# Column sums of w_mod from its natural 112-row chunks, a new order of work up to the first sums over tokens, and small VectorE operations set apart

## The chip, the cores and the metric

The kernel runs on one core of a Trainium2 chip. The metric is the device time of one execution in microseconds (us); lower is better. The engines are TensorE (PE in the profile; PEld is its weight load), VectorE (DVE), ScalarE (ACT), GpSimd (POOL) and SyncE (SP), which issues most of the loads. Each engine has its own list of instructions and works through it in order; semaphores make one engine wait for another.

## The reference

An adaLN-conditioned block: linear attention, then an MLP that mixes tokens. S = 2048 tokens, D = 448 channels, 16 heads of 28, F = 1792.

```
mod = silu(c) @ w_mod                     # w_mod: 448 x 2688, six vectors of 448
sa, ca, ga, sb, cb, gb = mod in six parts
h = layernorm(x) * (1 + ca) + sa
q, k, v = h @ wqkv                        # 448 x 1344
phi(t) = where(t > 0, t + 1, exp(t)) + 1e-6
kv = sum over tokens of phi(k) v;  z = sum over tokens of phi(k)
x = x + ga * ((phi(q) kv) / (phi(q) z + 1e-6)) @ wo
h = layernorm(x) * (1 + cb) + sb
x = x + gb * (gelu(h^T @ w1 + b1) @ w2 + b2)^T
```

## The kernel before

All is float32. TensorE's fast format, fp32r, keeps fewer bits, so most operands are cut into a high and a low half (ScalarE makes the high half by a copy, VectorE the low half by a subtraction) and a product is three matmuls: high by high, high by low, low by high. The order of each engine's instructions is the order in which the program writes them; it was laid out by hand, and nothing reorders it.

**Tiles.** The tokens are 16 tiles t of 128. `XT[t]` is a tile transposed (channels on the partitions, `load_xt`), `X[t]` the tile as it is (`load_x`). Channels come in chunks of 128, 128, 128 and 64. All big tiles come from one pool of 74 slots ("slots").

**The start.** Layernorm is folded into the weights: for the projections the raw x is multiplied by the weight rows scaled with 1 + ca, and the mean is taken off by an additional row. So the first thing that is needed is column j = 1 of `mod`, channels on the partitions: `col[1]`. The program loads c, then `w_mod`'s part for j = 1 in four blocks of rows (`load_first`, L148 to 152: 128, 128, 128 rows, and the last 64 rows folded in two halves, 128 x 256, laid out by the host in an input of its own). While the loads are under way TensorE runs nine matmuls on ones (`keep_warm(WARM)`, L181). `silu(c)` is made by ScalarE and VectorE (L187 to 191). `col_mm` (L218, L220) multiplies a block by silu(c), repeated, and so sums over its rows: five instructions for a set of 448 columns. For j = 1 it runs on block 0 and block 1, and then on the sum `acc` of blocks 2 and 3, which VectorE has made (`col_acc`, L204 and L211). Five more matmuls on ones follow (`keep_warm(5)`). `col_out` (L226) takes the result out of the PSUM bank. For j = 0, later, VectorE folds all four blocks (L206, L208, L211) and `col_mm` runs once.

**Weights.** `w_high` (L256, `wh`) scales a chunk of the k weights with `col[1]` and rounds it; `w_low` (L268, `wl`) makes the low half. `w_row`, `row_part` (L274, L276), `row_sum` (L283), `row_bias` (L286) and `row_out` (L290, L291) make the rows that stand for the mean and for sa.

**Projections.** `a_split(t)` cuts `XT[t]` into `hh` (L400) and `hl` (L403). `project(t, 1)` is ten matmuls (L420, `kp`): three each for chunks 0 to 2, one for chunk 3, whose low parts lie in the free half of the partitions. For tiles 0 and 1 the twenty matmuls are in an order of their own (`projects`). `close(t)` (L427) adds the rows of mean and rest, for which the tile's statistics must have been transposed (`a_rows` L383 and L385, `a_transpose` L393, `a_copy` L396).

**Statistics.** Mean and variance of a tile come either from ScalarE in two passes (`a_stats_act`, L351 and L330) or from VectorE (`a_stats_dve`, L367 and L368); GpSimd makes the powers (`a_pow`, L342). Before the change tiles 0 to 3 are ScalarE's.

**Sums over tokens.** `a_exp` (L434, L435) and `a_pk` (L440) make phi(k); `a_pk_parts` cuts it into `pkh` (L488) and `pkl` (L490, or for most tiles L492 with an adding DMA from GpSimd, L493). `a_norm`, `a_high`, `a_low` make the normalized tile in two halves `xh`, `xl`. `a_outer(t)` (L514, `cacc`) adds a tile's products to four PSUM banks: eleven matmuls, of which seven use `pkh` and four `pkl`.

**Order around the change.** After the start the program is a straight list by hand down to a loop over t = 4 to 15, in which each step projects tile t + 1, closes tile t, adds tile t - 4 to the sums, makes statistics three tiles ahead, cuts `XT[t + 3]`, and does a piece of the q weights and of `mod`. SyncE's loads are in one list too: c, w_mod for j = 1, xt0, the k weights, xt1, xt2, w_mod for j = 0, then x and xt in turns with the q weights between tile 5 and tile 6.

Of the kernel before, what the change touches and what calls it, by code (L numbers as in the profile page):

```python
# [8 lines left out]
F32 = mybir.dt.float32  # L9
# [41 lines left out]
def block_kernel(ctx: ExitStack, tc: tile.TileContext, x, xt, wqkv, wo, w1, b1, w2, b2, c, wmod, wfirst, out):  # L51
# [67 lines left out]
    c_sb = cst.tile([P, 8], F32, name="c_sb")  # L119
    nc.sync.dma_start(c_sb, c)  # L120
    X = [None] * NT
# [11 lines left out]
    wm = {}  # L133

    def load_mod(j):
        for k in range(4):
            wm[j, k] = (tslot if j == 5 else slot)(f"wm{j}_{k}", parts=G)
            nc.sync.dma_start(wm[j, k], wmod[k * G:(k + 1) * G, j * D:(j + 1) * D])

# [8 lines left out]
    def load_first(j):  # L148
        for k in range(4):
            w = D if k < 3 else 256  # L150
            wm[j, k] = slot(f"wm{j}_{k}", w)
            nc.sync.dma_start(wm[j, k], wfirst[j, :, k * D:k * D + w])
# [9 lines left out]
    load_x(1)  # L162
# [6 lines left out]
    load_qkv(0)  # L169
    load_xt(6)  # L170
    load_x(6)
    for t in (7, 8):
        load_xt(t)
        load_x(t)
# [11 lines left out]
    ec = cst.tile([P, 8], F32, name="ec")  # L186
    nc.scalar.activation(ec, c_sb, AF.Exp, scale=-1.0)  # L187
    sc = cst.tile([P, 8], F32, name="sc")
    nc.vector.tensor_scalar_add(ec, ec, 1.0)
    nc.vector.reciprocal(ec, ec)  # L190
    nc.vector.tensor_mul(sc, c_sb, ec)
    mods, macc = {}, {}
# [6 lines left out]
    one = ones[:, 0:1]  # L199

    def col_acc(j):
        acc = macc[j] = slot(f"acc{j}")
        if j:
            nc.vector.tensor_scalar_mul(acc, wm[j, 2], sc[:, 2:3])  # L204
        else:
            nc.vector.tensor_scalar_mul(acc, wm[j, 0], sc[:, 0:1])  # L206
            for k in (1, 2):
                nc.vector.scalar_tensor_tensor(acc, wm[j, k], sc[:, k:k + 1], acc, op0=ALU.mult, op1=ALU.add)  # L208
        for r, (c0, c1) in enumerate(((0, 256), (256, D))):
            p = slice(r * 64, (r + 1) * 64)  # L210
            nc.vector.scalar_tensor_tensor(acc[p, c0:c1], wm[j, 3][p, :c1 - c0], sc[p, 3:4], acc[p, c0:c1],  # L211
                                           op0=ALU.mult, op1=ALU.add)

    def col_mm(ps, a, b, first, last):
        b = b.to_broadcast([P, P])
        for ch in range(4):
            n = P if ch < 3 else 64
            nc.tensor.matmul(ps[:n, ch * P:(ch + 1) * P], a[:, ch * P:ch * P + n], b, start=first and ch == 0,  # L218
                             stop=last, skip_group_check=True)
        nc.tensor.matmul(ps[64:, 384:512], a[:, 384:D], b, start=False, stop=last, skip_group_check=True)  # L220

    def col_out(j, ps):
        col[j] = cst.tile([P, 4], F32, name=f"col{j}")
        ps = ps.rearrange("p (c n) -> p c n", n=P)[:, :, 0]
        if j == 1:
            nc.vector.tensor_scalar_add(col[j], ps, 1.0)  # L226
        else:
            nc.vector.memset(col[j], 0.0)
            nc.vector.tensor_copy(col[j][:, :3], ps[:, :3])
            nc.vector.tensor_copy(col[j][:64, 3:4], ps[:64, 3:4])  # L230

    def mod_part(j, k):
        if k == 0:
            macc[j] = (tslot if j == 5 else slot)(f"acc{j}", parts=G)
            nc.vector.tensor_scalar_mul(macc[j], wm[j, 0], sc[:G, 4:5])
        else:
            nc.vector.scalar_tensor_tensor(macc[j], wm[j, k], sc[:G, 4 + k:5 + k], macc[j], op0=ALU.mult, op1=ALU.add)
# [88 lines left out]
    junk = slot("junk")  # L326
# [35 lines left out]
    def a_stats_dve(ts):  # L362
        g, ve = a_group(ts)

        def one(i):
            b6 = small.tile([P, 6], F32, name=f"st{ts[i]}", tag="st")
            nc.vector.bn_stats(b6, X[ts[i]])  # L367
            nc.vector.bn_aggr(mv[ts[i]][:, 0:2], b6)  # L368
# [4 lines left out]
        return one, end  # L373

    def a_stats(t):
        one, end = a_stats_dve((t,))
        one(0)
        end()

    def a_rows(t):  # L380
        r = rowst[t % RING]
        pair = mv[t][:, 0:2]
        nc.vector.tensor_copy(r[:, 64:].rearrange("p (b c) -> p b c", b=2)[:, :, 0:2],  # L383
                              pair.unsqueeze(1).to_broadcast([P, 2, 2]))
        nc.vector.tensor_sub(r[:, 66:68], pair, r[:, 64:66].bitcast(F32))  # L385
# [46 lines left out]
    def a_exp(t, ps):  # L432
        eks[t] = (slot(f"ek{t}"), slot(f"rk{t}"))
        nc.scalar.activation(eks[t][0], ps, AF.Exp, scale=mv[t][:, 2:3])  # L434
        nc.scalar.activation(eks[t][1], ps, AF.Relu, scale=mv[t][:, 2:3])  # L435
# [69 lines left out]
    def a_outer(t):  # L505
        if not cacc:
            cacc.extend(bank(f"cacc{ch}") for ch in range(4))
        xh, xl = xss.pop(t)
        kh, kl = pks.pop(t)
        for ch in range(4):  # L510
            s = slice(ch * P, (ch + 1) * P)
            todo = [(xh, kh), (xh, kl)] + ([(xl, kh)] if ch < 3 else [])
            for i, (a, b) in enumerate(todo):
                nc.tensor.matmul(cacc[ch][:, :D], a[:, s], b, start=(t == 0 and i == 0),  # L514
                                 stop=(t == NT - 1 and i == len(todo) - 1))

    pc = bank("col1")
    for k in range(2):
        col_mm(pc, wm[1, k], sc[:, k:k + 1], k == 0, False)
    nc.scalar.activation(sel_s, sel_f, AF.Copy)  # L520
    col_acc(1)
    a_split(0)
    col_mm(pc, macc.pop(1), one, False, True)
    keep_warm(5)
    col_out(1, pc)
    for ch in (3, 0, 1, 2):
        w_high(1, ch)
        w_low(1, ch)
    a_split(1)
    a_split(2)  # L530
    projects([(0, "hh", 0), (0, "hl", 0), (0, "hh", 3), (0, "hh", 1), (0, "hl", 1), (0, "wl", 0), (0, "hh", 2),
              (0, "hl", 2), (0, "wl", 1), (1, "hh", 0), (1, "hh", 1), (1, "hh", 2), (1, "hh", 3), (0, "wl", 2),
              (1, "wl", 0), (1, "wl", 1), (1, "wl", 2), (1, "hl", 0), (1, "hl", 1), (1, "hl", 2)], 1, "kp")
    project(2, 1, "kp")
    w_row(1)
    act01, end01 = a_stats_act((0, 1))
    act01(0)
    col_acc(0)
    pc = bank("col0")
    col_mm(pc, macc.pop(0), one, True, True)  # L540
    row_sum(1)
    a_split(3)
    act01(1)
    end01()
    col_out(0, pc)
    for ch in range(4):
        row_part(1, ch)
    a_rows(0)
    a_rows(1)
    project(3, 1, "kp")  # L550
    a_transpose(0, 2)
    row_bias(1)
    a_split(4)
    a_norm(0)
    dve45, end45 = a_stats_dve((4, 5))
    dve45(0)
    act23, end23 = a_stats_act((2, 3))
    act23(0)
    act23(1)
    end23()  # L560
    a_copy(0)
    a_copy(1)
    row_out(1)
    a_rows(2)
    a_rows(3)
    a_high(0)
# [5 lines left out]
    project(4, 1, "kp")  # L572
    a_split(5)
    a_low(0)
    kps = [close(t, 1) for t in (0, 1)]
    a_transpose(2, 2)
    project(5, 1, "kp")
    a_exp(0, kps[0])
    a_pk(0, kps[0])
    dve45(1)  # L580
    end45()
    a_copy(2)
    a_copy(3)
    kps += [close(t, 1) for t in (2, 3)]
    a_exp(1, kps[1])
    a_norm(1)
    a_pk_parts(0)
    a_outer(0)
    a_pk(1, kps[1])
    a_rows(4)  # L590
    a_rows(5)
    a_transpose(4, 2)
    a_exp(2, kps[2])
    a_split_high(6)
    a_pk(2, kps[2])
    a_split_low(6)
    a_exp(3, kps[3])
    a_high(1)
    a_copy(4)
    a_copy(5)  # L600
    project(6, 1, "kp")
    kps.append(close(4, 1))
    a_stats(6)
    a_pk_parts(1)
    a_low(1)
    a_rows(6)
    a_pk(3, kps[3])
    a_pk_parts(2)
    a_stats(7)
    wo_sb = []  # L610
    late = [t for t in range(NT) if t not in Q_EARLY.values()]
    for t in range(4, NT):
# [12 lines left out]
        if t == 12:  # L625
            mp = mod_sum2(2)
        if 4 < t < NT - 2:
            a_rows(t + 2)
        if 5 <= t < 9:
            w_low(0, t - 5)  # L630
            row_part(0, t - 5)
        if 7 < t + 3 < NT:
            a_stats(t + 3)
# [4 lines left out]
        if t + 3 < NT:  # L638
            a_split_high(t + 3)
# [6 lines left out]
        if t + 3 < NT:  # L646
# [524 lines left out]
_INS = ['A_x', 'xt', 'qkv', 'A_wo', 'B_w1', 'b1', 'B_w2', 'b2', 'c', 'B_wmod', 'first']  # L1171
# [3 lines left out]
def lay_out(inputs):  # L1175
# [12 lines left out]
    col = np.zeros((P, 8), c.dtype)  # L1188
    for k in range(3):
        col[:, k] = c[k * P:(k + 1) * P]  # L1190
    col[:64, 3] = col[64:, 3] = c[3 * P:]
    for k in range(4):
        col[:G, 4 + k] = c[k * G:(k + 1) * G]
    a['c'] = col
    a['B_wmod'] = a['w_mod']
    first = np.zeros((2, P, 3 * D + 256), c.dtype)
    for j in range(2):
        m = a['w_mod'][:, j * D:(j + 1) * D]
        for k in range(3):
            first[j, :, k * D:(k + 1) * D] = m[k * P:(k + 1) * P]  # L1200
        first[j, :64, 3 * D:] = m[3 * P:, :256]
        first[j, 64:, 3 * D:3 * D + 192] = m[3 * P:, 256:]
    a['first'] = first
# [24 lines left out]
```

## Time and profile before

| | us |
|---|---|
| three runs | 444.47, 444.76, 445.54 |
| median | 444.76 |
| the profiled execution | 445.22 |
| its span | 443.5 |
| PE busy in the span | 436.6 (98%) |
| DVE busy | 364.7 (82%) |
| ACT busy | 273.3 (62%) |
| POOL busy | 110.0 (25%) |

The span is the time from the first to the last instruction of the profiled execution; 1.7 us of its time lie around it. The profile's page gives the busy time of each engine, the span in 40 slices, the DMA queues, and the chain of work that ended last, which is followed back from the last instruction: at each step to what released it, or to the instruction ahead of it on its engine. The trace behind the page is asked for that chain in order of time (start, us, engine, tile and line, and how many instructions), for the busy time in stretches of the span, for the instructions in order of time (with the idle time ahead of one in brackets, and what ended it), and for all instructions that touch one tile. A float32 matmul (`warm`, `col`) leaves two records, an fp32r one (`kp`, `cacc`) one.

### The profile page before, as it was taken

To read this page: it belongs to the slowest core of one execution; us is meant where nothing else is said; L and a number is where in the kernel's file an instruction comes from. 1 tells how busy PE (TensorE), PEld (TensorE's weight loads), DVE (VectorE), ACT (ScalarE), POOL (GpSimd) and SP (SyncE) were. 2 spreads that over 40 slices of the span, in tenths; PEclk is the share of its full clock that TensorE was granted. 3 is DMA by queue.
4 is the path that set the end of the run, shared out by engine and by line. 5 is a ranking of instruction groups with operands and counts; after the bars stand their busy time and mean duration, and the time that the engine had idled before them with its cause. 6 is when DMAs were issued, how large, how long until landed. Compare 5 with 4: busy or idle time off the path is not lost.

```text
span 443.5 us, 7249 instructions
## 1 busy us (share of the span) xinstructions
PE 436.6 (98%) x2392; PEld 404.4 (91%) x2392; DVE 364.7 (82%) x811; ACT 273.3 (62%) x572; POOL 110.0 (25%) x195
## 2 busy tenths in 40 slices
PE   8999999999999999999999999999999999999995
PEld 7878899999899999989999999999999999999995
DVE  3989996689998899896468975829699998898892
ACT  3889877648656776767664354617375555645550
POOL 3227563200025355554300000010102331132010
PEclk9999999999999999999999999999999999999999
DMA  7998999545100004322328652478369978995332
GB/s 256 381 290 171 237 225 217 106 152 173 58 0 1 24 25 102 67 49 47 120 63 249 220 165 89 138 201 225 68 190 206 207 171 176 216 184 112 61 41 43
DMA packets 62294, 63.47 MB, mean 143 GB/s; under 512 B 4720, under 2 KB 54576, under 8 KB 62256
## 3 DMA queue, kind: packets, MB, share of 16 engines
q1 hardware_dynamic: 54048, 49.79, 37.3%
q0 software_dynamic: 8208, 13.21, 18.9%
q8 instruction: 19, 0.31, 0.3%
q14 instruction: 19, 0.16, 0.1%
HBM read 45.88 MB, written 7.34 MB: 120 GB/s over the span
## 4 chain that ended last, share of the span: by engine, by line
PE 93%; ACT 3%; DVE 2%; POOL 1%; issue 1%; ACTq 0%
PE y L1024 19%; PE up L838 10%; PE up L837 10%; PE up L836 9%; PE y L1025 9%; PE cacc L514 7%; PE qp L420 7%; PE op L785 7%; PE kp L420 6%; PE tq L769 1%; PE col L218 1%; PE warm L181 1%; PE qp L427 1%; PE kvb L725 1%; PE rowb L283 1%; PE wp L853 1%
## 5 line engine op out<-in xcount | busy, mean ns | idle before, releaser
L838 PE MATMUL up<-h2h,pl 128*128 128x448 f32 x224 | 81.4, 364 | 0.0
L837 PE MATMUL up<-h2l,ph 128*128 128x448 f32 x224 | 81.3, 363 | 0.0
L836 PE MATMUL up<-h2h,ph 128*128 128x448 f32 x224 | 80.9, 361 | 0.0
L986 POOL DMA_DIRECT2D a<-a x16 | 14.1, 960 | 142.7 <-DVE u L950 76.9
L837 PEld LDWEIGHTS up<-h2l,ph 128*128 128x128 f32 x224 | 42.1, 188 | 3.2
L836 PEld LDWEIGHTS up<-h2h,ph 128*128 128x128 f32 x224 | 42.0, 187 | 2.9
L838 PEld LDWEIGHTS up<-h2h,pl 128*128 128x128 f32 x224 | 42.1, 188 | 2.3
L83 DVE TENSOR_TENSOR pl<-pr,ph 128x512 fp32r<-128x512 f32 x52 | 34.6, 686 | 3.1 <-ACT ph L82 2.3
L82 ACT ACTIVATE ph<-pr 128x512 fp32r<-128x512 f32 x52 | 31.2, 626 | 3.3 <-PE up L837 2.6
L1030 ACT ACTIVATE cc<-y 128x448 f32<-128x448 f32 x24 | 12.9, 544 | 23.7 <-PE y L1025 23.7
L1044 POOL DMA_DIRECT2D out_dram<-yt x15 | 13.6, 908 | 48.6 <-DVE yt L1035 38.1
L514 PE MATMUL cacc<-pkh,xh 128*128 128x448 f32 x64 | 24.4, 382 | 0.3 <-ACT pkh L488 0.3
L785 PE MATMUL op<-wph,pth 112*128 112x448 f32 x64 | 24.5, 382 | 0.0
L950 DVE TENSOR_TENSOR u<-u,mod 128x448 f32<-128x448 f32 x14 | 8.7, 621 | 18.8 <-ACT u L949 18.6
L514 PE MATMUL cacc<-pkl,xh 128*128 128x448 f32 x64 | 23.3, 364 | 0.2 <-DVE pkl L490 0.2
L949 ACT ACTIVATE u<-up,b1c 128x448 f32<-128x448 f32 x14 | 8.7, 624 | 23.9 <-PE up L838 21.9
L420 PE MATMUL kp<-wh,hh 128*128 128x448 f32 x64 | 23.2, 373 | 0.2 <-ACT wh L256 0.2
L420 PE MATMUL qp<-wh,hh 128*128 128x448 f32 x64 | 23.3, 364 | 0.0
L785 PE MATMUL op<-wpl,pth 112*128 112x448 f32 x64 | 23.2, 363 | 0.0
L785 PE MATMUL op<-wph,ptl 112*128 112x448 f32 x64 | 23.2, 363 | 0.0
L773 ACT ACTIVATE pth<-tq 112x512 fp32r<-112x512 f32 x16 | 9.6, 598 | 17.3 <-PE tq L769 17.3
L827 ACT ACTIVATE y<-y,nb,rt 128x448 f32<-128x448 f32 x16 | 12.1, 758 | 11.8 <-POOL nb L826 11.8
(231 smaller groups left out, 1357.9 us busy)
## 6 DMA issues: line engine op xcount, KB each, us to landing
pr<-in_B_w_dram SPq DMA_DIRECT2D x56, 256.0 KB, 3.1
a<-in_B_w_dram SPq DMA_DIRECT2D x32, 256.0 KB, 4.8
a<-in_B_w_dram SPq DMA_DIRECT2D x32, 192.0 KB, 4.7
xt<-in_xt_dram SPq DMA_DIRECT2D x16, 256.0 KB, 4.8
x<-in_A_x_dram SPq DMA_DIRECT2D x16, 224.0 KB, 4.8
out_dram<-x SPq DMA_DIRECT2D x15, 224.0 KB, 2.5
out_dram<-yt POOLq DMA_DIRECT2D x15, 224.0 KB, 5.2
wm<-in_B_wmod_dram SPq DMA_DIRECT2D x16, 196.0 KB, 4.8
```

Of the source, the lines that this page charges most:

```text
L82: nc.scalar.activation(hi, full, AF.Copy)
L83: nc.vector.tensor_sub(lo, full, hi.bitcast(F32))
L420: nc.tensor.matmul(pps[t, j][:, :D], a[:, ch * P:(ch + 1) * P], w, start=first, stop=False)
L514: nc.tensor.matmul(cacc[ch][:, :D], a[:, s], b, start=(t == 0 and i == 0), stop=(t == NT - 1 and i == len(todo) - 1))
L785: nc.tensor.matmul(opb[t][:, :D], a[:, s], b, start=(n == 0), stop=(n == 11))
L836: nc.tensor.matmul(ps[:, :D], hi[:, sl], mh, start=first, stop=False)
L837: nc.tensor.matmul(ps[:, :D], hi[:, sl], ml, start=False, stop=False)
L838: nc.tensor.matmul(ps[:, :D], lo[:, sl], mh, start=False, stop=last)
L986: nc.gpsimd.dma_start(w, a, accum_op=ALU.add)
L1024: nc.tensor.matmul(ps[:, :D], h[:, s], w, start=opens and r == 0, stop=False, skip_group_check=True)
L1025: nc.tensor.matmul(ps[:, :HD], l[:, s], wh, start=False, stop=closes and r == PAIRS - 1, skip_group_check=True)
L1044: nc.gpsimd.dma_start(of[t * P:(t + 1) * P, :], ysum.pop(t), accum_op=ALU.add)
```

## The change

In `block_kernel` and in the host's layout:

- The host's array `first` is gone, and c comes as 4 columns instead of 8. Both column sums use w_mod in its natural chunks of 112 rows (`G`), four for each j, as the other vectors do.
- For j = 1, ScalarE issues the loads of chunks 0 and 1, SyncE that of c and then of chunks 2 and 3.
- `col_acc` folds chunks 2, 0 and 1 on VectorE, for both j. `col_mm` runs on chunk 3 alone and on the fold: ten instructions for a j. For j = 1 chunk 0 of the columns is finished and taken out first, and `wh` of chunk 0 is begun ahead of the others. The five matmuls on ones are gone.
- The loads are in another order: x0 and x1 ahead of w_mod for j = 0, the q weights behind tile 7, and the loads of tiles 9 and 10 and of w_mod for j = 2 later.
- From the first projection to the loop the list is in a new order: tiles 0 and 1 have their statistics on VectorE, the splits of tiles 4 to 7 come earlier, projection 4 is cut around the first two closing matmuls, `pkh` of tile 0 comes between the two activations of tile 1, and the first sum runs its seven products with `pkh` ahead of the four with `pkl`.
- Two small VectorE operations of which the second needs the first get others between them: `a_rows` for two tiles at once, and in the loop `apart`, which takes from two lists in turns.

```diff
+    load_mod(1, (0, 1), nc.scalar)
+    c_sb = cst.tile([P, 4], F32, name="c_sb")
     nc.sync.dma_start(c_sb, c)
+    load_mod(1, (2, 3))
...
-    load_first(1)
     load_xt(0)
-    load_qkv(1, chs=(3, 0, 1, 2))
+    load_qkv(1)
     load_xt(1)
     load_xt(2)
-    load_first(0)
     load_x(0)
+    load_x(1)
+    load_mod(0)
     load_xt(3)
...
     def col_acc(j):
+        acc = macc[j] = slot(f"acc{j}", parts=G)
+        nc.vector.tensor_scalar_mul(acc, wm[j, 2], sc[:G, 2:3])
+        for k in (0, 1):
+            nc.vector.scalar_tensor_tensor(acc, wm[j, k], sc[:G, k:k + 1], acc, op0=ALU.mult, op1=ALU.add)
+
+    def col_mm(j, todo):
+        fresh = ("col", j) not in col
+        if fresh:
+            col["col", j] = bank(f"col{j}")
+        ps = col["col", j]
+        for ch, k in todo:
+            a, b = (macc[j], ones[:G, 0:1]) if k is None else (wm[j, k], sc[:G, k:k + 1])
             n = P if ch < 3 else 64
+            for p in (0, 64)[:1 if ch < 3 else 2]:
+                nc.tensor.matmul(ps[p:p + n, ch * P:(ch + 1) * P], a[:, ch * P:ch * P + n], b.to_broadcast([G, P]),
+                                 start=fresh, stop=k is None, skip_group_check=True)
+                fresh = False
...
+    def apart(*lists):
+        lists = [list(l) for l in lists]
+        while any(lists):
+            for l in lists:
+                if l:
+                    l.pop(0)()
...
-            for i, (a, b) in enumerate(todo):
+            for i, (a, b) in enumerate(todo[::1 if t else 2]):
...
+        if t == 0:
+            for ch in range(4):
+                nc.tensor.matmul(cacc[ch][:, :D], xh[:, ch * P:(ch + 1) * P], kl, start=False, stop=False)
...
-    pc = bank("col1")
-    for k in range(2):
-        col_mm(pc, wm[1, k], sc[:, k:k + 1], k == 0, False)
+    col_acc(1)
+    col_mm(1, [(ch, 3) for ch in range(4)] + [(0, None)])
     nc.scalar.activation(sel_s, sel_f, AF.Copy)
-    col_acc(1)
-    a_split(0)
-    col_mm(pc, macc.pop(1), one, False, True)
-    keep_warm(5)
-    col_out(1, pc)
-    for ch in (3, 0, 1, 2):
+    a_split_high(0)
+    col_out(1, (0,))
+    col_mm(1, [(ch, None) for ch in (1, 2, 3)])
+    w_high(1, 0)
+    a_split_low(0)
+    col_out(1, (1, 2, 3))
+    w_low(1, 0)
+    for ch in (1, 2, 3):
         w_high(1, ch)
         w_low(1, ch)
     a_split(1)
     a_split(2)
...
+    dve01, end01 = a_stats_dve((0, 1))[:2]
+    dve01(0)
+    dve01(1)
+    end01()
     col_acc(0)
     a_split(3)
+    col_mm(0, [(ch, k) for k in (3, None) for ch in range(4)])
+    act23, end23 = a_stats_act((2, 3))
+    act23(0)
+    a_rows(0, 1)
+    a_split_high(4)
+    act23(1)
+    end23()
+    a_norm(0)
+    col_out(0, range(4))
     for ch in range(4):
         row_part(1, ch)
     project(3, 1, "kp")
+    row_sum(1)
     a_transpose(0, 2)
     row_bias(1)
+    a_split_low(4)
+    a_split_high(5)
     a_copy(0)
     a_copy(1)
+    tail = [(4, kind, ch) for ch in range(3) for kind in ("hh", "wl", "hl")] + [(4, "hh", 3)]
+    projects(tail[:6], 1, "kp")
+    a_split_low(5)
+    dve45, end45 = a_stats_dve((4, 5))[:2]
+    dve45(0)
+    a_high(0)
     row_out(1)
+    a_split_high(6)
+    kps = [close(t, 1) for t in (0, 1)]
+    projects(tail[6:], 1, "kp")
+    a_exp(0, kps[0])
...
+        apart(rows, stats[:2] + rest[:1] + stats[2:] + rest[1:])
```

More of the change, by code (lines that the diff above doesn't have):

```diff
@@ L168, in block_kernel @@
     load_x(5)
[L169 removed]
     load_xt(6)
     load_x(6)
[L172 to L174 removed]
+    load_xt(7)
+    load_x(7)
+    load_qkv(0)
+    load_xt(8)
+    load_x(8)
     warm = bank("warm")
@@ L198, in block_kernel @@
     col = {}
-    one = ones[:, 0:1]
     def col_acc(j):
[L202 to L212, printed above, removed]
@@ L214, in col_mm @@
-    def col_mm(ps, a, b, first, last):
-        b = b.to_broadcast([P, P])
-        for ch in range(4):
-            n = P if ch < 3 else 64
[L218 to L224, printed above, removed]
+        acc = macc[j] = slot(f"acc{j}", parts=G)
@@ L225, in col_out @@
+    def col_out(j, chs):
+        c0, c1 = chs[0], chs[-1] + 1
+        if j not in col:
+            col[j] = cst.tile([P, 4], F32, name=f"col{j}")
+        ps = col["col", j].rearrange("p (c n) -> p c n", n=P)[:, :, 0]
         if j == 1:
-            nc.vector.tensor_scalar_add(col[j], ps, 1.0)
+            nc.vector.tensor_scalar_add(col[j][:, c0:c1], ps[:, c0:c1], 1.0)
         else:
@@ L363, in a_stats_dve, with first, second @@
         g, ve = a_group(ts)
+        b6 = {}
+        def first(i):
+            b6[i] = small.tile([P, 6], F32, name=f"st{ts[i]}", tag="st")
+            nc.vector.bn_stats(b6[i], X[ts[i]])
+        def second(i):
+            nc.vector.bn_aggr(mv[ts[i]][:, 0:2], b6[i])
         def one(i):
-            b6 = small.tile([P, 6], F32, name=f"st{ts[i]}", tag="st")
-            nc.vector.bn_stats(b6, X[ts[i]])
-            nc.vector.bn_aggr(mv[ts[i]][:, 0:2], b6)
+            first(i)
+            second(i)
         def end():
@@ L372, in end, with a_rows_high, a_rows_low, a_rows @@
             a_pow(g, ve)
-        return one, end
+        return one, end, first, second
     def a_stats(t):
-        one, end = a_stats_dve((t,))
+        one, end = a_stats_dve((t,))[:2]
         one(0)
         end()
-    def a_rows(t):
+    def a_rows_high(t):
+        nc.vector.tensor_copy(rowst[t % RING][:, 64:].rearrange("p (b c) -> p b c", b=2)[:, :, 0:2],
+                              mv[t][:, 0:2].unsqueeze(1).to_broadcast([P, 2, 2]))
+    def a_rows_low(t):
         r = rowst[t % RING]
[L382 to L385, printed above, removed]
+        nc.vector.tensor_sub(r[:, 66:68], mv[t][:, 0:2], r[:, 64:66].bitcast(F32))
+    def a_rows(*ts):
+        for t in ts:
+            a_rows_high(t)
+        for t in ts:
+            a_rows_low(t)
+    def apart(*lists):
[4 more added lines that the diff above has]
+                    l.pop(0)()
     tps = {}
@@ L567, in block_kernel @@
+    a_pk(1, kps[1])
+    kps += [close(t, 1) for t in (2, 3)]
+    a_norm(1)
+    a_outer(0)
+    a_exp(2, kps[2])
+    a_stats(6)
     load_xt(9)
@@ L1187, in lay_out @@
     c = a['c'].reshape(D)
[L1188 to L1193, printed above, removed]
+    col = np.zeros((P, 4), c.dtype)
+    col[:G] = c.reshape(4, G).T
     a['c'] = col
     a['B_wmod'] = a['w_mod']
[L1196 to L1203, printed above, removed]
     return a
```

120 lines of the change are left out of this document (41 added, 79 removed).

## The prediction

> **What bounds the kernel now.** I read the page's chain first, then the chain of work in order of time, then the busy times by stretches, and last the timeline of the first 45 us.
>
> ```profile
> PE 93%; ACT 3%; DVE 2%; POOL 1%; issue 1%; ACTq 0%
> ```
>
> The chain that ends last is TensorE for 93% of the span. So a change counts only where it makes TensorE begin earlier, wait less, or do less. The stretches show where it can:
>
> ```profile
> 11.00:42.00 31.00, 30.08 (x149) 25.59 (x150) 28.49 (x77) 28.29 (x66) 12.39 (x16) 1.00 0.95 285
> 42.00:100.00 58.00, 58.00 (x292) 53.22 (x292) 48.96 (x123) 42.40 (x83) 21.51 (x25) 1.00 0.84 190
> 183.00:200.00 17.00, 16.83 (x92) 15.38 (x91) 15.09 (x35) 11.27 (x24) 8.82 (x20) 1.00 0.29 63
> ```
>
> The columns are the length, then PE, PEld, DVE, ACT and POOL busy, then clock, DMA share and GB/s. From 42 us on TensorE is busy all the time, and even the stretch around 190 us, where the chain runs over other engines for a while, leaves it idle for only 0.17 us. What the start gains or loses is therefore handed on to the end nearly one to one. The place to work it out is the chain up to the end of the third sum over tokens (`cacc`), at 39.57 + 2.21 = 41.78 us:
>
> ```profile
> 1.11 4.21 PE warm L181 x18
> 5.32 1.53 PE col L218 x7
> ...
> 8.20 1.12 PE col L218 x7
> ...
> 9.48 0.17 DVE col L226
> ...
> 9.68 1.24 ACT wh L256 x2
> ...
> 10.96 6.28 PE kp L420 x30
> 17.24 0.92 PE col L218 x7
> ...
> 18.28 1.58 PE rowb L283 x7
> 19.86 2.01 PE kp L420 x10
> 21.87 0.25 PE rw L393 x2
> 22.12 0.75 PE rowb L286 x2
> 22.87 2.01 PE kp L420 x10
> 24.88 0.22 PE kp L427
> ...
> 27.99 0.47 ACT pkh L488
> ...
> 28.49 0.64 DVE pkl L490
> ...
> 29.17 2.28 PE cacc L514 x10
> ...
> 36.72 0.61 DVE hl L403
> ...
> 37.38 1.88 PE kp L420 x8
> 39.26 0.20 PE kp L427
> 39.46 0.11 PE rw L393
> 39.57 2.21 PE cacc L514 x11
> ```
>
> Three things are to be seen. The first projection matmul (`kp`) starts at 10.96. From there to 24.88 the chain stays on TensorE. Behind that it leaves TensorE several times: for the exponentials and the halves `pkh`, `pkl` ahead of the first sum, and for `hl` ahead of the next projection. How much time those exits hold: from 24.88 to 41.78 are 16.90 us. TensorE's own work there is three projections (5, 6, 7) at 2.01, seven closing matmuls (`kp` L427) at 0.20, three sums at 2.21, and six transposes (`rw`), four of them in pairs at 0.25 and two at 0.11: 6.03 + 1.40 + 6.63 + 0.72 = 14.78. So the **gaps are 2.12 us**. That, and the time before 10.96, is all that this change can win.
>
> **The change part by part.** First the start, up to the column sums.
>
> ```profile
> 1.24 1.84 SPq L152 DMA_DIRECT2D wm<-in_first_dram  x4
> ...
> 6.86 0.45 DVE L204 TENSOR_SCALAR acc<-wm,sc 128x448 f32<-128x448 f32 x1 [3.11 <-DMA wm<-in_first_dram]
> ...
> 7.35 0.93 DVE L211 SCALAR_TENSOR_TENSOR acc<-wm,sc,acc 64x256 f32<-64x256 f32 x2
> ...
> 9.68 2.35 ACT L256 ACTIVATE wh<-wr,col 128x448 fp32r<-128x448 f32 x4 [1.27 <-DVE col L226]
> ...
> 14.57 1.40 DVE L208 SCALAR_TENSOR_TENSOR acc<-wm,sc,acc 128x448 f32<-128x448 f32 x2
> ```
>
> Now SyncE issues c and then the four vectors, 1.84/4 = 0.46 us apart; the third vector lands at about 6.8 (VectorE waits for it until 6.86). After the change SyncE issues c and vectors 2 and 3, and ScalarE vectors 0 and 1. No row shows a load issued by ScalarE. The bounds: best, the two queues work side by side and the last of four lands about two issues (0.92) plus its share earlier, at 5.4; worst, the two loads wait behind the table load and land no sooner than the last one now, at 7.3 (VectorE takes it at 7.35). I take 6.3, in the middle, and keep both ends.
>
> From there by the new order: five matmuls on vector 3 (a set of five column sums takes 8.20 to 9.46, 1.25), to 7.55. Beside them VectorE folds vectors 2, 0 and 1 (0.45 + 1.40), hidden unless vector 1 is the last to land. Then one column sum on the folded vectors, with its result seen after about 0.45 (8.0), `col_out` of chunk 0 (0.17 and a hand-over, 8.2), four more matmuls (0.8 of a set and its tail, 1.15: 9.35), `col_out` of the others (9.55). I let the four wait for the first `col_out`, since both touch one PSUM bank; without that wait the result is 0.4 earlier. `wh` of chunk 0 is made meanwhile. Then ScalarE makes `wh` 1 to 3 and `hh` of token tile 1: four operations of 0.59 (2.35 for four): **11.9, say 12.0**. Seven matmuls of tile 0 run before that in the shadow of ScalarE; the other 23 of the 30 start at 12.0.
>
> A cover is removed here: the ten records of `keep_warm(5)` that stood between the column sums and the first `kp`. As time on TensorE it cost nothing, because `wh` was being made; what it may cost to lose is the second rival.
>
> The rest, from 12.0 on, as TensorE's own time: 23 matmuls, 6.28 - 7 x 0.20 = 4.88; the column sums for j = 0, now ten instructions instead of five, 2 x 1.04 = 2.08 (17.24 to 18.28 is 1.04); row sums 1.58; projection 3, 2.01; transposes 0.25; row bias 0.75; projection 4, 2.01; and the 14.78 from above. Sum 28.34, so 40.34 with no gap left.
>
> What becomes of the gaps? The first sum now runs its seven products with `pkh` first (1.4 us) and covers the 0.64 of `pkl`; `pkh` of tile 0 goes between the two activations of tile 1; the splits of tiles 4 to 7 are made one projection earlier. That should take out most. What is late next is VectorE, busy 28.49 of 31 us. Its load:
>
> ```profile
> L367 DVE BATCH_NORM_STATS2 st<-x x5: 619/620/622, 22.6 to 39.1; 128x6 f32<-128x448 f32 x5
> L330 ACT ACTIVATE junk<-x,as x4: 667/670/673, 15.2 to 21.2; 128x448 f32<-128x448 f32 x4
> ```
>
> The statistics of tiles 0 and 1 go from ScalarE (two passes over each tile, one of them this row of 0.67, so over 2.4 freed there) to VectorE (0.62 and a small one, 1.8 for both). The fold for j = 0 loses its two half-height operations (0.93). The small pairs cost:
>
> ```profile
> 21.05 0.16 DVE L383 CAST rowst<-mv 128x4 fp32r<-128x4 f32 x1
> ...
> 21.25 0.16 DVE L385 TENSOR_TENSOR rowst<-mv,rowst 128x2 fp32r<-128x2 f32 x1
> ...
> 21.32 0.16 DVE L383 CAST rowst<-mv 128x4 fp32r<-128x4 f32 x1
> ```
>
> The second needs the first and starts 0.20 after it; the third needs neither and starts 0.07 after the second. With another operation between, I count 0.13 saved a pair, 0.9 for seven pairs. VectorE's net is about 0, and it starts its split work a little earlier than now. I leave **0.8 us of gaps**: the closing matmul of tile 0 still waits for ScalarE and VectorE to make the bias rows from `rowb`, and `hl` of tile 8 is as tight as now. Bounds 0.2 and 2.12. That gives 41.1 against 41.78: **0.6 us earlier**.
>
> Moved loads, at no cost: the second column set moves behind x0 and x1, but its fold comes only after the statistics of tiles 0 and 1. The q weights go behind tile 7; their first use is in step 4 of the loop, behind everything reckoned above. The loads of tiles 9 and 10 are issued later in the program, for this use:
>
> ```profile
> 22.54 0.33 SPq L131 DMA_DIRECT2D xt<-in_xt_dram  x1
> ...
> 43.24 0.63 ACT L400 ACTIVATE hh<-xt 128x512 fp32r<-128x512 f32 x1
> ```
>
> There are 20 us between issue and use; if they slip by more than about 15, `hh` of tile 9 would be the new wait. In the steady loop the small operations apart save VectorE time that TensorE, never idle after 42 us, doesn't ask for: nothing.
>
> The vectors' landing is where a rule speaks against the change. "DMA: Bandwidth & Descriptors" in the Trainium skill, section "Issuing engines are not separate DMA queues", says that issuing from several engines saves only the issuing time. By it the last vector would land near the worst end, the sum would be the third rival's, and no row here shows the split either way.
>
> **The rivals.**
>
> *Faster (0.20).* The two queues really run side by side and all four land by 5.4: the same steps from 5.4 give about 11.1 to 11.3 for the start; with 0.4 to 0.8 us of gaps that is 11.2 + 28.34 + 0.6 = 40.1 against 41.78, 1.7 us earlier: **443.1**. It decides from a last landing before about 5.7. For it: SyncE's 0.46 an issue is what staggers the loads at the start. Against it: in 5.3 to 7.0 us the DMA engines are full, the next to last column, so the bytes may bound.
>
> ```profile
> 5.30:7.00 1.70, 1.70 (x12) 1.31 (x11) 0.14 (x1) 0.00 (x0) 0.00 (x0) 1.00 0.98 304
> ```
>
> *Slower, by slow matmuls (0.27).* The same matmul (`warm`) comes twice, 18 records at the very start (in the chain above) and ten here:
>
> ```profile
> 9.36 1.38 PE L181 MATMUL warm<-ones 128*128 128x128 f32 x10
> ```
>
> Spaced, that is 4.21/18 = 0.234 against 0.138, 1.7 times. The column sums tell when it changes: 1.53/7 = 0.219 from 5.32, 1.12/7 = 0.16 from 8.20. So the fast form comes at 6.8 or a little later, after some 5.6 us without a break. In the changed kernel TensorE is out of work at 5.32 until vector 3 lands, then has 1.25, 0.3 and 0.9 us of work with waits between, and no `keep_warm(5)`. If matmuls fall back to, or stay in, the slow form when the projections begin, 5.6 us at 1/1.7 speed do 3.3 us of work: 2.3 lost. 0.6 gained and 2.3 lost: 1.7 slower, **446.5**; half as long a stay, 445.3. The point from which it decides is the break at 5.32: under some tenths it does nothing. "TensorE: Matmul & The Clock Gate" in the Trainium skill, Part 1, says that the array goes to full rate only after a busy window of about 3.4 us and back after an idle one; by it short breaks wouldn't throw it back, but could keep it from getting there. The 0.234 agrees that there is such a start.
>
> *No gain, by late vectors (0.08).* ScalarE's loads land together at 7.3. Then both folds on them stand on the path (1.40), the folded column sum starts at 8.7 instead of 7.55, and everything moves by 1.1: 42.2 against 41.78: **445.2**.
>
> *The gaps stay (0.07).* VectorE, with 1.8 us more of statistics, is the bound and the new order only moves the waits: 12.0 + 28.34 + 2.12 = 42.46, 0.7 later: **445.4**.
>
> **How the numbers follow.** The profiled execution took 445.22, of which 443.5 is the span; the median of the three runs is 444.76, 0.46 below. I take the difference from the median: 444.76 - 0.6 is **444.2** (rounded), chance 0.38, own range 443.6 to 444.9. The measurement of this kernel can tell about 0.3% (1.3 us) from no change. Faster by more: the faster rival, 0.20. Slower by more: the longer stays in the slow form, 0.23 (nearly all of that rival). Within: the rest, 0.57. The range goes from the faster rival to the long stay, 443.1 to 446.5; beyond it I leave 0.1 on either side.
>
> **What would show it.** Right: the last vector landed by about 6.3, the 8th `kp` at about 12.0, no `pkl`, `pkh` or `hl` in the chain between 25 and 40 us, ten `col` instructions in a row near 17 us, and the third sum ending near 41.1. Wrong: `kp` spaced by more than 0.2 in its first 5 us (slow form), `wm` waits of VectorE or TensorE to 7 us, or `DVE` entries that still hold a quarter of the chain between 25 and 40. A shift that is seen at 42 us and gone at the end would break the argument that the start is handed on one to one.

## The result, and the profile after

The changed kernel took **448.11 us** in the median of 10 runs (446.14 to 449.4), the kernel before 445.31 (10 runs beside it, 444.47 to 445.61): ratio **1.0061 [1.0049, 1.0073]** (in brackets the 95% interval), slower by 0.6% and clear of the noise. Its times spread over 3.3 us, those of before over 1.1. The profiled execution was one of its quickest: 446.38, span 444.7.

The page of the changed kernel, its shares of the chain and then busy times and granted clock:

```profile
PE 86%; DVE 5%; DMA 3%; ACT 2%; POOL 2%; issue 1%; SPq 0%; DVEq 0%; POOLq 0%
...
PE 436.8 (98%) x2382; PEld 403.6 (91%) x2382; DVE 363.9 (82%) x815; ACT 270.7 (61%) x562; POOL 110.2 (25%) x193
...
PEclk8999999999999999999999999999999999999998
```

TensorE has 2382 matmul instructions, ten fewer than before (436.6 us), and still 436.8 us of work: some of it ran slowly. The chain of the changed kernel in order of time (start, length, what), to the third sum:

```profile
1.70 4.51 DMA wm<-in_B_wmod_dram
6.34 1.71 PE col L212 x12
8.08 0.17 DVE col L222
8.29 1.60 PE col L212 x8
9.89 7.48 PE kp L437 x30
17.37 2.28 PE col L212 x20
19.65 2.21 PE kp L437 x10
...
25.16 0.63 DVE wrow L287
...
29.69 0.53 DVE pkl L509
...
32.22 1.01 POOL mv L337
...
34.48 0.62 DVE pkl L509
...
35.76 2.08 PE cacc L533 x9
37.84 2.00 PE kp L437 x10
...
40.16 2.20 PE cacc L533 x11
```

The projections start 1.1 us earlier than before (9.89 for 10.96), but the first thirty take 7.48 us in place of 6.28. From about 24 to 35.7 us the chain is on VectorE, ScalarE and GpSimd. The third sum ends at 42.36 (before 41.78): 0.58 late. Why the first products are slow stands in TensorE's timeline and in the clock column (the third from the right) of the busy times by stretches, both of the changed kernel:

```profile
6.34 1.28 PE L212 MATMUL col<-sc,wm 112*128 112x128 f32 x10 [1.03 <-DMA wm<-in_B_wmod_dram]
...
9.82 0.74 PE L437 MATMUL kp<-wh,hh 128*128 128x448 f32 x1
10.36 0.58 PE L437 MATMUL kp<-wh,hl 128*128 128x448 f32 x1
```
```profile
5.19:8.60 3.41, 2.13 (x15) 1.55 (x15) 2.04 (x5) 0.96 (x2) 0.00 (x0) 1.00 1.06 358
8.60:12.01 3.41, 3.41 (x13) 2.33 (x12) 2.19 (x5) 2.21 (x5) 0.00 (x0) 0.50 1.06 365
```

For 3.41 us, from 8.60 to 12.01, the granted clock is 0.50. In the 3.41 us ahead of it TensorE was at work for 2.13.

Half of the loss of this execution comes much later. Call lag how much later a matmul starts than the same one, matched by tile, in the profile of before. It is 0.50 to 0.56 us from 60 to 317 us, and 1.12 from 337 us to the end. In between, in the product stage (`y`), VectorE waits for the transfers with which GpSimd adds one block of `a` to another in memory. The same operation before, and in the changed kernel:

```profile
317.31 0.56 DVE L992 TENSOR_TENSOR s<-a,a 128x384 f32<-128x384 f32 x1 [0.51 <-DMA a<-a]
```
```profile
318.83 0.56 DVE L1015 TENSOR_TENSOR s<-a,a 128x384 f32<-128x384 f32 x1 [1.15 <-DMA a<-a]
```

1.52 us later, of which 0.55 had been brought along. The DMA queues around it: before, from 312 to 314.3 us, and the changed kernel, from 314.3 to 318.2 (packets, MB, share; the last line is from issue to landing):

```profile
q0 software_dynamic: 17, 0.03, 8.7%
q8 instruction: 1, 0.02, 2.9%
...
a<-a POOLq DMA_DIRECT2D x1, 192.0 KB, 3.9
```
```profile
q0 software_dynamic: 286, 0.46, 71.8%
q8 instruction: 1, 0.02, 1.4%
...
a<-a POOLq DMA_DIRECT2D x1, 192.0 KB, 5.1
```

One packet of 16 KB on the instruction queue (q8), program code, comes before the accumulating transfers (q0) in the first kernel and amid them in the second, and there the transfer lands 5.1 us after its issue, not 3.9.

### The profile page after: what moved, and what is told of

The parts are those of the page before. It is cut to its first block, busy times and chain, and to the rows that moved or that the text cites. A ratio compares the mean times of both kernels' runs of the same rounds, so it can differ in the third digit from the quotient of the medians.

```text
span 444.7 us, 7222 instructions
## 1 busy us (share of the span) xinstructions
PE 436.8 (98%) x2382; PEld 403.6 (91%) x2382; DVE 363.9 (82%) x815; ACT 270.7 (61%) x562; POOL 110.2 (25%) x193
## 4 chain that ended last, share of the span: by engine, by line
PE 86%; DVE 5%; DMA 3%; ACT 2%; POOL 2%; issue 1%; SPq 0%; DVEq 0%; POOLq 0%
PE y L1047 16%; PE up L859 9%; PE up L861 9%; PE up L860 9%; PE y L1048 8%; PE cacc L533 7%; PE qp L437 7%; PE op L808 7%; PE kp L437 6%; PE tq L792 1%; PE col L212 1%; DMA a<-a 1%; DMA a<-in_B_w_dram 1%; DMA wm<-in_B_wmod_dram 1%; PE qp L444 1%
## 5 line engine op out<-in xcount | busy, mean ns | idle before, releaser
L437 PE MATMUL kp<-wh,hh 128*128 128x448 f32 x64 | 24.2, 383 | 0.0
L533 PE MATMUL cacc<-pkl,xh 128*128 128x448 f32 x60 | 21.8, 364 | 0.0
L337 POOL TENSOR_TENSOR mv<-ve,roots 128x2 f32<-128x2 f32 (+1 forms) x13 | 13.9, 1069 | 27.9 <-DVE ve L374 27.7
```

Source lines behind the costliest of these rows:

```text
L337: nc.gpsimd.tensor_tensor(g[:, :, 1:3], ve, roots.unsqueeze(1).to_broadcast([P, n, 2]), op=ALU.pow)
L437: nc.tensor.matmul(pps[t, j][:, :D], a[:, ch * P:(ch + 1) * P], w, start=first, stop=False)
```

## The experiments

Three theories, and a fourth that the first traces suggested. **Clock**: the new start leaves TensorE idle long enough for the granted clock to fall. **Order**: the new list itself is slower. **Late**: what is lost behind 300 us comes from other places of the buffers in memory. **Code**: TensorE's code comes in pieces, and a program with another number of instructions meets them elsewhere. Each ratio is to runs of the kernel before taken beside it.

**The changed kernel again.**

> The changed kernel itself, once more, for a second profile. Its ten times lie between 446.1 and 449.4 us, and the first profile, at 446.4, is one of the fast ones: granted clock 0.50 from 9.4 to 10.9 us, first 30 projection matmuls 7.48 us long instead of 6.28. Clock theory (TensorE's clock is low for part of the first projections, for a length that differs from run to run): a time of some 448, with the 30 matmuls 1 to 3 us longer than in the kernel before, and the lag behind it already full at 42 us. Order theory (the new list up to the first sums is itself slower): the lag at 42 us is the same 0.6 as in the first profile, whatever the time. Late theory (new places in the pool delay loads near the end): half a microsecond or more is added behind 300 us, as in the first profile (0.57 there).

447.82 (4 runs, 446.19 to 448.3), 1.0053 [1.0039, 1.0068]. In its profile the clock never falls and the third sum ends at 41.79, as before; yet the lag at 337 us is 0.75. So there are two losses, of which this execution has one. Of the ten executions of this kernel above 447.5 us, in the two sets of runs, five have a mean granted clock of 0.990 or 0.991, where the kernel before reads 0.997 to 1.000; the other five read 0.997 to 1.000 too. None of the ten has a trace, so what the last five went through isn't recorded.

**Fills in the new start.**

```diff
-WARM = 9
+WARM = 11
...
-    projects([(0, "hh", 0), (0, "hl", 0), (0, "wl", 0), (0, "hh", 1), (0, "hl", 1), (0, "hh", 2), (0, "hl", 2),
-              (1, "hh", 0), (0, "wl", 1), (1, "hh", 1), (1, "hh", 2), (0, "wl", 2), (0, "hh", 3), (1, "wl", 0),
+    projects([(0, "hh", 0), (0, "hl", 0)], 1, "kp")
+    keep_warm(3)
+    projects([(0, "wl", 0), (0, "hh", 1), (0, "hl", 1), (0, "hh", 2), (0, "hl", 2)], 1, "kp")
+    keep_warm(2)
+    projects([(1, "hh", 0), (0, "wl", 1), (1, "hh", 1), (1, "hh", 2), (0, "wl", 2), (0, "hh", 3), (1, "wl", 0),
```

> The changed kernel with TensorE kept busy at the start: two more matmuls on ones ahead of the column sums, three behind the first two projection matmuls, two behind the seventh. Clock theory: the granted clock stays at 1.00 behind 7 us and the 30 matmuls are no longer than what their operands allow; time 444.0 to 445.5, and the spread between runs falls from 3 us to 1. Order theory and late theory: still 447 to 449, since neither is touched.

445.55 (12 runs, eleven of them within 445.4 to 445.83, one at 448.66, which stays unexplained), 1.0016 [1.0004, 1.0028]. Clock 1.00 throughout, third sum at 42.15; the lag is 0.29 us at 62 and 0.42 at 337. Nearly all of the loss is gone, the late part too, with every buffer in its new place: the late theory falls. The fills do not close the wait for the last vector. In this profile it is still open, and the clock holds:

```profile
5.30:7.00 1.70, 0.35 (x3) 0.38 (x4) 1.54 (x3) 0.00 (x0) 0.00 (x0) 1.00 1.05 348
```

**The old start with the new list, and the new start with the old list.** Each takes the start (vectors, their loads, column sums) from one kernel, the list and the loop from the other. Against the changed kernel and against the kernel before:

```diff
-    load_mod(1, (0, 1), nc.scalar)
+    load_first(1)
...
-    col_acc(1)
-    col_mm(1, [(ch, 3) for ch in range(4)] + [(0, None)])
+    pc = bank("col1")
+    for k in range(2):
+        col_mm(pc, wm[1, k], sc[:, k:k + 1], k == 0, False)
```
```diff
-    load_first(1)
+    load_mod(1, (0, 1), nc.scalar)
...
-    keep_warm(5)
-    col_out(1, pc)
+    col_out(1, (0,))
+    col_mm(1, [(ch, None) for ch in (1, 2, 3)])
```

> The new list from the first projections on, the new order of loads and the small operations apart, but the start of the kernel before: four blocks loaded by SyncE, its column sums, its five matmuls on ones and its order of the first twenty projection matmuls. Clock theory: no low clock in the first projections; the new list takes out some 1.3 of the 2.1 us of gaps, so 443.5 to 444.5. Order theory: 447 to 448, as the changed kernel. Late theory: 0.5 us above what the third sum's end at 42 us would give.

445.6 (11 runs), 1.0007 [0.9998, 1.0015].

> The start of the changed kernel (natural chunks, two of them loaded by ScalarE, column sums chunk by chunk for both j, no five matmuls on ones, its order of the first twenty) with the list and loop of the kernel before. Clock theory: low clock in the first projections, the whole loss or more of it: 447 to 449.5, with the wide spread. Order theory: 444.5 to 446, only the second set of column sums for j = 0 (1.0 us) and the start's own gain. Late theory: as the kernel before behind 300 us.

447.36 (5 runs), 1.0048 [1.0035, 1.0061]. The loss comes with the start, and it is both losses at once: this mix has 2382 matmul instructions like the changed kernel, e3_oldstart 2392 like the one before. The new start's profile with the old list shows two low stretches in a row, and a third sum at 44.52, 2.74 late; another 0.84 is added between 317 and 337 us:

```profile
8.20:13.00 4.80, 4.60 (x15) 3.36 (x16) 3.29 (x7) 3.17 (x6) 0.00 (x0) 0.50 1.07 312
13.00:17.00 4.00, 4.00 (x17) 3.67 (x17) 3.46 (x7) 3.31 (x9) 0.00 (x0) 0.76 1.06 359
```

And in e3_oldstart the new list gains nothing: it has lost the waits for `pkh` and `hl`, but TensorE's waits there from 17 to 42 us are two others, the third sum ending at 41.92:

```profile
PE col L221 <- DVE acc L214: 1.0, 1, 1.0
PE kp L451 <- DVE wrow L294: 0.4, 1, 0.4
```

The second is in the changed kernel too. The first comes from the mix, in which the old single column set for j = 0 waits for VectorE's fold; the changed kernel doesn't have it, so this run doesn't show what the new list alone is worth.

**Before without its fill.**

```diff
-    keep_warm(5)
```

> The kernel before without its keep_warm(5), ten matmuls of about 0.115 us that fill TensorE's wait at 9.5 to 10.9 us; nothing else changes. Prediction's step (they cost and save nothing): 445.2, as before. Clock theory (TensorE idle for over a microsecond lets the granted clock fall to 0.50 for 3.4 us): 445.2 in some executions and 1 to 3 us more in others. Code theory (TensorE's own code comes in pieces of 16 KB at places fixed by how many instructions went before; with ten matmuls fewer a piece that came at 312.5 us comes at about 316, beside the accumulating transfers of the product stage, and y waits for them): the quick executions too are 0.6 to 0.9 late, 445.9, with a piece of code between 314 and 318 us, the 192-KB transfer landing 5.1 us after its issue in place of 3.9, and the lag arising between 318 and 334 us.

446.1 (12 runs, 445.1 to 447.79), 1.0024 [1.0014, 1.0034]. The stretches of its profile:

```profile
9.40:10.90 1.50, 0.20 (x1) 0.21 (x2) 0.75 (x2) 1.48 (x3) 0.00 (x0) 1.00 1.06 405
10.90:14.40 3.50, 3.50 (x11) 3.14 (x11) 3.46 (x7) 2.46 (x5) 0.00 (x0) 0.52 1.06 385
```

TensorE idle for 1.3 us, then 3.4 us at half clock; lag 1.34 at 28 us and, with a piece of code at 317.0, 2.61 at 337. This one execution, the slowest of the twelve, has both losses, from taking five matmuls (ten instructions) that ran in idle time out of the old kernel.

**The same fill in fewer instructions.** Each two fill matmuls of 128 columns become one of 256.

```diff
-        for i in range(n):
-            nc.tensor.matmul(warm[:, :P], ones, ones, start=True, stop=True)
+        while n:
+            m = 2 if n > 1 else 1
+            nc.tensor.matmul(warm[:, :m * P], ones, ones[:, 0:1].to_broadcast([P, m * P]), start=True, stop=True)
+            n -= m
```

In e1_fill:

> The changed kernel with the fills of e1_fill, but each pair of fill matmuls of 128 columns made one of 256 columns: the same TensorE time in the fills, 14 matmul instructions fewer, so as many as in the changed kernel. Clock theory alone: the same as e1_fill, 445.55. Code theory: the clock stays full, but the code piece comes at about 316 us again, so 446.1 to 446.4, with the 192-KB accumulating transfer at 5.1 us and 0.6 to 0.9 us of lag between 318 and 334 us.

446.55 (5 runs, 446.31 to 447.32), 1.0036 [1.0024, 1.0048]: 1.0 above e1_fill. Clock 1.00, lag 0.06 to 0.08 up to 315 us, 1.26 at 337, with the code amid the transfers (314.3 to 318.2 us):

```profile
q8 instruction: 1, 0.02, 2.4%
...
a<-a POOLq DMA_DIRECT2D x1, 192.0 KB, 5.2
```

In the kernel before, nothing else changed:

> The kernel before with nothing changed but its fill matmuls: each pair of 128 columns is one of 256, the same TensorE time in twelve matmul instructions fewer (2380 in place of 2392). Clock theory and the prediction: 445.2, as before. Code theory: full clock, no lag up to 315 us, then a code piece between 313 and 318 us beside the accumulating transfers, 0.6 to 1.0 us of lag by 334 us, 445.9 to 446.2.

446.9 (8 runs, 445.58 to 447.56), 1.003 [1.0019, 1.0042]. In its profile (447.56) the clock stays at 1.00 while TensorE works and the lag is -0.11 at 317 us and 1.08 at 337. That execution lost another 1.3 at the very end, more than the expectation had: from 438 us on a piece of code lies beside the stores of the output. It and then the kernel before, in the same stretch:

```profile
q8 instruction: 1, 0.02, 0.9%
...
out_dram<-yt POOLq DMA_DIRECT2D x1, 224.0 KB, 5.2
out_dram<-xb SPq DMA_DIRECT2D x1, 112.0 KB, 3.9
```
```profile
out_dram<-yt POOLq DMA_DIRECT2D x1, 224.0 KB, 3.9
out_dram<-xb SPq DMA_DIRECT2D x1, 112.0 KB, 2.6
```

The code theory stands: only TensorE's instruction count was touched, and the transfers that a piece meets land 1.2 to 1.4 us later than the same ones before. All fourteen profiles go by the count: the six with 2380 or 2382 matmul instructions lose 0.56 to 1.22 us between 317 and 337 us, the seven others with 2392 or 2396 at most 0.12 against the kernel before. It is no price for every piece: in the kernel before, other 192-KB transfers of this kind take 3.8 to 6.2 us with no piece beside them. That the piece and the transfer share one of the DMA engines is only argued; it wasn't tried. And the times of this run spread over 2.0 us with every fill kept, so a spread alone doesn't tell the two losses apart.

**The smallest mending, and who issues the loads.** The changed kernel with the first line of this edit alone, then with both.

```diff
-WARM = 9
+WARM = 14
...
-    load_mod(1, (0, 1), nc.scalar)
+    load_mod(1, (0, 1))
```

> The changed kernel with WARM 14 in place of 9 and no other fill: ten matmuls more ahead of the first column sums, TensorE at work until the vectors land, but with its waits among the first ten projections still open. Clock theory by the wait at 5.3 to 6.3 us: clock stays full, and, since the ten matmuls also put the code piece back to about 312.5 us, 445.6. If the waits at 7.5 to 11.5 us alone can drop the clock: some executions at 446 to 448. Code theory alone: all executions 0.6 below the changed kernel's, 447.2 in the median.

445.88 (11 runs, 444.86 to 445.96), 1.0012 [1.0004, 1.0021].

> e8_warm14 with all four of the first vectors issued by SyncE, one after the other at 0.44 us each, in place of two by ScalarE. Two more issues of 0.44 us put the third and fourth vector and everything behind them 0.9 us later at the issue. If the landing is set by the issue: fourth vector at about 7.1, third sum up to 0.9 later, 446.4. If the transfers themselves set it: fourth vector at 6.2 to 6.5, 445.9 as in e8_warm14.

445.63 (11 runs, 445.22 to 446.06), 1.0007 [0.9998, 1.0016]. Filling the wait at 5.3 us is enough: with the waits among the first products still open, none of these 22 executions took more than 446.06. It isn't shown to be the only cure, since e1_fill left that wait open (1.40 us in its profile) and filled the others. Both runs also have 2392 matmul instructions, so they mend the late loss as well. And with SyncE alone the fourth vector, in the chain of e10_sp, lands at 6.54, where the changed kernel has 6.21:

```profile
2.64 3.90 DMA wm<-in_B_wmod_dram
```

Four profiles with two loads issued by ScalarE (the changed kernel, e4_newstart, e6_wide, e1_fill) have 6.21, 6.32, 6.30 and 6.51, so no delay clear of this spread is shown, and none shows in the time.

**One column set for j = 0, the old list with a filled new start, and a further order.** All three sum the second vectors on VectorE. The edit is that of e9_oldlist, against the changed kernel's code; e7_one sets the split of tile 3 between the folds, and moves `project(3)` up:

```diff
-        for k in (0, 1):
+        for k in (0, 1) if j else (0, 1, 3):
...
-    col_mm(0, [(ch, k) for k in (3, None) for ch in range(4)])
+    col_mm(0, [(ch, None) for ch in range(4)])
```

> e1_fill with WARM 14, and the second vectors summed wholly on VectorE first (one set of ten column matmuls in place of two, one VectorE operation of 0.7 us more), with the projection of tile 3 ahead of those matmuls, the bias of the row matrix behind six products of tile 4, and three products of tile 5 ahead of the two waiting closes. It has 2392 matmul instructions like the kernel before. If TensorE is what bounds 17 to 42 us: 1.1 us less work and the 0.4 us wait for wrow covered, third sum at 41.0, 444.3 to 444.6. If VectorE's chain of statistics bounds it: third sum at 41.8 to 42.3, 445.2 to 445.8.

445.63 (11 runs), 1.0013 [1.0005, 1.0022]; third sum at 42.42, nearer to VectorE's side of the alternative, in an execution whose clock rose late (7.0 us).

> The kernel before with the new start only (first vectors in natural chunks, their loads, the new load order), WARM 14 and the fills of e1_fill, the second vectors summed wholly on VectorE, and the list and loop of the kernel before; 2392 matmul instructions. With clock full and code piece at about 312.5 us this shows what the earlier start is worth by itself. Prediction's view (the eighth first-tile product at 12.0 in place of 12.5 is handed on one to one): third sum at 41.3, 444.7. Load theory (the products behind the eighth wait for tiles and halves that the loads bring no sooner): third sum at 41.7 to 41.9, 445.1 to 445.4.

445.5 (11 runs), 1.0005 [0.9996, 1.0014]; third sum at 41.71. The first product starts 1.36 earlier than before, the eighth at 12.27, only 0.21 earlier. ScalarE's timeline in e9_oldlist shows why:

```profile
9.91 1.79 ACT L249 ACTIVATE wh<-wr,col 128x448 fp32r<-128x448 f32 x3 [0.68 <-DVE col L219]
11.61 1.13 ACT L393 ACTIVATE hh<-xt 128x512 fp32r<-128x512 f32 x2
```

Three `wh` wait for the second column result, and `hh` of tile 1 stands behind them.

```diff
-    keep_warm(3)
-    projects([(0, "wl", 0), (0, "hh", 1), (0, "hl", 1), (0, "hh", 2), (0, "hl", 2)], 1, "kp")
-    keep_warm(2)
-    projects([(1, "hh", 0), (0, "wl", 1), (1, "hh", 1), (1, "hh", 2), (0, "wl", 2), (0, "hh", 3), (1, "wl", 0),
+    keep_warm(2)
+    keep_warm(3, 32)
+    projects([(0, "wl", 0), (0, "hh", 1), (0, "hl", 1), (0, "hh", 2), (0, "hl", 2), (0, "wl", 1), (0, "wl", 2),
+              (1, "hh", 0), (1, "hh", 1), (1, "hh", 2), (0, "hh", 3), (1, "wl", 0),
```

> e9_oldlist with the first tile's two products with the low parts of the weights ahead of the second tile's first product, so that these two no longer stand behind ScalarE's rounding of the second tile (done at 12.1), and the second fill dropped for three matmuls of 32 columns; the number of instructions stays. If ScalarE's order is what held the first products: the run of products that starts at 12.4 starts some 0.4 earlier in the list, third sum at 41.2 to 41.4, 444.7. If the VectorE and ScalarE chains behind 24.8 us hold it anyway: third sum at 41.7, 445.3 to 445.5.

445.12 (11 runs) beside 445.29, 1.0 [0.9991, 1.0008]: no difference from before, and no kernel here beats it. In its profile, its slowest execution (445.74), the first thirty products end earlier, and projection 2 begins 0.11 early, but the transposes then wait for the statistics on GpSimd (`mv`) and start 0.19 late; third sum at 42.12:

```profile
19.85 1.50 POOL mv L335
21.38 0.18 DVE rowst L376
...
21.89 0.56 PE rw L386 x2
```

## Why the prediction was wrong

Forecast 444.2 against 448.11, above the range's 446.5. The prediction's base, 444.76, was low too (445.31 in the runs beside the changed kernel); as a change it said 0.6 us faster, and measured is 2.80 slower. By its steps:

- **The last vector at 6.3**: right, 6.21. The table load held nothing back: ScalarE issued at 1.09 while it ran. The late-vectors rival didn't come about; its landing at 7.3 did not come even with SyncE alone (6.54). The rule cited there (the Trainium skill, "DMA: Bandwidth & Descriptors", "Issuing engines are not separate DMA queues") isn't contradicted: dividing the issues moved the landing by 0.33 us at most, about as much as the four profiles with the split differ among themselves (0.30).
- **The eighth `kp` at 12.0**: right where the clock held (11.91 in the second profile of the changed kernel, 12.07 in e6_wide), 12.50 where it fell. Before it was 12.48, so even at full clock only about half a microsecond was gained there.
- **No cost for TensorE's idle time in the new start**: the failed step. Of the removed `keep_warm(5)` the prediction said "As time on TensorE it cost nothing", and the forecast put the clock that can be lost at nothing. The slow-matmul rival had the mechanism and the break at 5.32, but a chance of 0.27 and a price of 2.3 at once. Half clock comes in pieces of 3.4 us: none in one profile of the changed kernel (third sum 0.01 late), one in the other (0.58), two in e4_newstart (2.74). That short breaks would not throw the clock back, as the prediction took from the rule, didn't hold. In the kernel before the removal of `keep_warm(5)` alone did it (e2_nokeep); in the changed kernel filling the break at 5.32 was enough, with `keep_warm(5)` still gone (e8_warm14). In medians it is 2.80 - 1.48 = 1.3: the changed kernel's distance from before less that of e6_wide, which has fills and the same count of instructions.
- **0.8 us of gaps left**: mis-sized. In e6_wide the third sum ends at 41.93, 29.86 behind the eighth `kp`, where 28.34 were TensorE's own: 1.5 left. Of the 2.12 that the prediction wanted to shorten, only 0.92 was time without a matmul, by its own row from 11 to 42 us (31.00 less 30.08); in e6_wide it is 0.56 from 12 to 42 us. The gaps-stay rival was right in kind: VectorE's operations stand in the chain from 25 to 35 us. At full clock list and start together put the third sum 0.01 to 0.37 late (the second profile, e6_wide, e1_fill), not 0.6 early.
- **Handed on one to one to the end**: true from 42 to 317 us, false behind. The code piece, in no rival, adds 1.48 - 0.36 = 1.1 in medians (e6_wide less e1_fill); the changed kernel's own two profiles lost 0.56 and 0.72 there.

So the three parts are 0.4 for list and start with the fills, 1.1 for the code piece and 1.3 for the clock. They add up to 2.8 because each is a difference of neighbours in one row of medians, taken in different sets of runs; how the loss of the slow executions divides between clock and code stays open within about half a microsecond. The second column set for j = 0 cost about what was said (2.28 us for 2.08); the moved loads and the small operations apart were not tried alone, and no trace shows a cost or a gain of theirs.

## What to carry to other kernels

Matmuls that fill an idle stretch near the start are not free to remove: here they held the clock, and without them the times of several executions spread. A spread can have another cause too (e12_bwide), so look at the clock in a trace. Whenever the number of an engine's instructions changes, look along the whole trace for where the lag changes, not only at the edited stage; one fill more or less can move a piece of code onto or off a transfer that something waits for. Here an earlier first matmul was worth nothing (e9_oldlist), since the engine that feeds the next ones was hardly earlier.

## What the runs showed of the hardware

The low clock comes in stretches of 3.41 us (8.60 to 12.01 in the changed kernel, 11.03 to 14.44 in e2_nokeep; twice that in e4_newstart, from 8.07) and not in every execution of a kernel. In the 3.41 us ahead of these three TensorE had 2.13, 1.64 and 2.02 us of work. Little work alone doesn't decide: e1_fill had 2.02 in a stretch as long, and its clock stayed:

```profile
4.11:7.53 3.42, 2.02 (x18) 1.74 (x17) 1.82 (x3) 0.47 (x2) 0.59 (x5) 1.00 1.04 331
```

What keeps the clock stays open. "TensorE: Matmul & The Clock Gate" in the Trainium skill, Part 1, speaks of a window of about 3.4 us and of a clock that falls after an idle one. The length agrees; but here the clock fell behind stretches that were half to two thirds busy, and the measurement decides. The clock column reads 1.00 ahead of its first change, also while the first `warm` matmuls run slowly (0.234 us each in the kernel before, 0.138 at 9.4 us), so a mean near 1 doesn't exclude a slow start. And a piece of code of 16 KB comes 19 times in the span; where one came amid the 192-KB transfer at 313 to 316 us, this landed 5.1 to 5.5 us after its issue instead of 3.9.
